# A transformer block with a product-key expert layer on one core: later searches queued behind the latest weighting, transposes of places set apart, block 0's places loaded during attention

## The chip, the core and the metric

The kernel runs on one core of a Trainium2 chip. The core has five engines, each with a queue of its own: PE (TensorE, matrix products and transposes; its weight loads are shown as PEld), DVE (VectorE), ACT (ScalarE), POOL (GpSimd) and SP (SyncE, which here issues nearly all DMAs). PE writes into PSUM, eight banks of 128 partitions x 2 KB; the others work between SBUF and PSUM. The metric is the device time of one execution in microseconds, the median of several runs.

## What is computed

N = 2048 tokens of width D = 448, one layer of attention (16 heads of 28) and one of experts, each behind a normalization and added to its input:

```
h  = x + softmax(q k^T / sqrt(28)) v @ wo          with q, k, v from layernorm(x) @ wqkv
xf = layernorm(h)
q1, q2 = halves of xf @ w_q                        (16 heads, 256 each)
s1, s2 = q1 @ k1^T, q2 @ k2^T                      (64 keys each)
t1, i1 = the 8 largest of s1;  t2, i2 = the 8 largest of s2
top_s, top_e = the 8 largest of the 64 sums t1 + t2, with expert numbers 64 * i1 + i2
g = softmax(top_s)
out = sum over heads and k of g * gelu(xf . u[top_e]) * v[top_e]       (4096 experts)
h2 = h + out
```

## The kernel before

The token axis is cut into four blocks of 512 tokens (b = 0 to 3), each of four groups of 128 (j). Instead of gathering rows of u and v for each token, the kernel computes all 4096 experts for all tokens, in 32 slices f of 128 experts, and multiplies by a dense matrix G of weights that is zero where an expert wasn't chosen. Products are made of half-precision parts (a high and a low part of each factor), so an up-projection of one slice and block is 11 matmuls of 128x512 (`mm_all`, L92) and the weighted sum is 12 matmuls of 128x448 per slice (L1194).

**Stages.** First the projections for q, k, v. Then attention, in 257 steps of a Python generator; into the same stretch are woven, by hand, the projection, the scores and the search for the best keys of token blocks 0, 1 and 2, and the splitting of u and v into parts. Then a short stage that projects block 3, keeps its key scores for later (`kept_scores`, in the 16 tiles `ring`) and builds the weights G of block 0. Then four expert blocks, one for each token block.

**Weaving.** `weave((generator, n, lo, hi), ...)` runs generators in turn: the n units of a generator get evenly spaced places between lo and hi, and the unit with the smallest place is traced next. A unit is what a generator does up to its next `yield`; an empty unit only takes a place.

**Queues.** Up to the end of the weights of block 0 the order of the woven text is the order of the queues (`manual_schedule`). In the expert blocks a compile-time scheduler orders each engine's queue: of the instructions that it takes to be ready, the first in the text. `tc.issue_after(ins)` forbids it to put what is traced inside ahead of `ins` on the engine of `ins`; it adds no wait at run time, and it binds only that engine's instructions.

**An expert block** (`experts`, L1172): 32 steps. Step f traces the up-projection of a slice some way ahead (`up`, PE then ACT's gelu, L1153, into one of four tiles of `ring` in block 0, of twenty later), the weighting of slice f+2 (`weigh`: DVE multiplies the gelu's result by G, L1167; ACT makes the high half of it, L1168; DVE makes the low half, L1169) and the 12 matmuls of slice f into the four PSUM banks `acc` (L1194). Blocks 1 to 3 begin with 19 up-projections made ahead (`ups`).

**Weights** (`weights(b)`, L936): loads the chosen places of block b from DRAM (`st` from `sd`, L940, its first unit), then for 32 chunks of 16 tokens makes on DVE indicator matrices (f1 L952, fg L958, p L973; two buffers of p, tag p1) and on PE their products (L1000 for block 0; L990 for the others), which go to G (L1002, or L993 on ACT and L994 on DVE). Of block b+1, the first chunks (EARLY: 11, 8, 11) are made during expert block b and the rest at the start of expert block b+1.

**Later searches** (`later`, L1210): what remains of the search is done in the expert blocks. In order: `pairs_of` for groups 2 and 3 of token block 2 (9 units each; the best 8 of 64 sums, with `found`: four times MAX8, L796, and four times FIND_INDEX8, L798, in a unit, then index arithmetic), `places_of` block 2 (9 units: `soften` on DVE and ACT, then `to_slots`: for each of four groups four transposes on PE, L903, into a PSUM tile of name M of which there are two, and two copies by ACT, L96 in the profile, then a store to `sd`), `bests` of block 3 (32 units of `found` on the kept scores), `pairs_of` for the four groups of block 3 and `places_of` block 3. LATER gives the units for expert blocks 0, 1 and 2, and SPLIT the share of the block over which they are spread; the first units of the next block's weights take the rest. All of them stand inside `behind(newest[0], ...)`, where `newest[0]`, read once when `later` is made, is the last p instruction of block 0's weights.

Of the kernel before, what the change touches and what calls it, by code (L numbers as in the profile page):

```python
# [60 lines left out]
def block(ctx: ExitStack, tc: tile.TileContext, x, wqk, wv, wo, wq, k12, uT, v, cst, out):  # L61
# [811 lines left out]
    PAIRS = 9  # L873
# [20 lines left out]
            if j % 2:  # L894
                yield

    def to_slots(eng, b):
        st = bg.tile([128, 2, 1024], F16, name="st", bufs=2)
        slots, gslots = st[:, 0].rearrange("p (k n) -> p k n", k=2), st[:, 1].rearrange("p (t k u) -> p t k u", k=2, u=2)
        for j in range(4):  # L900
            p = P[0].tile([128, 4, 128], F16, name="M")
            for k in range(4):
                nc.tensor.transpose(p[:, k], sl[j][:, k], ident16)  # L903
            copy(eng, slots[:, :, 128 * j:128 * j + 128], p[:, :2])
            copy(eng, gslots[:, 64 * j:64 * j + 64], p[:, 2:].rearrange("p k (t u) -> p t k u", u=2))
            yield
        nc.sync.dma_start(s_d[b], st)

    def places_of(b, eng):
        yield from soften()  # L910
        yield from to_slots(eng, b)

    PLACES = 9

# [5 lines left out]
    def behind(ins, gen):  # L920

        while True:
            with tc.issue_after(ins):
                if next(gen, end) is end:
                    return
            yield
# [130 lines left out]
    with tc.manual_schedule(engines={ET.PE, ET.DVE, ET.Activation, ET.Pool, ET.SP}):  # L1057
# [28 lines left out]
        for b in range(3):  # L1086
            t = begin[b] - FOLDED
            look = search(b, [(i, j) for g in ((0, 1), (2, 3)) for i in range(4) for j in g])
            work += [(project(b), PROJECT, t, t + PROJECT), (islice(look, 1), 1, t + 20, t + 21)]
            t += 26  # L1090
            p = 64 * b + 175 - FOLDED
            work += [(look, SEARCH, t, t + SEARCH)]
            if b < 2:
                work += [(chain(*[pairs_of(j, nc.gpsimd) for j in range(4)]), 4 * PAIRS_POOL, t + 18, p),
                         (places_of(b, nc.scalar), PLACES, p, p + 12)]
            else:
                work += [(pipeline([pairs_of(j, nc.gpsimd) for j in (0, 1)], 6), 6 + PAIRS_POOL, t + 20, 257 - FOLDED)]
        work += [(parts_of_up(14, 32), 18 + PART, 0, 40), (tops(VS, lambda f: v[:, f], D), TOPS, 6, 66), (VS.share(), 3, 67, 70), (scales(), 1, 73, 74),
                 (parts_of_down(0, 14), 14 + PART, 74, 120), (parts_of_down(14, 32), 18 + PART, 120, 180)]
        weave(*work)  # L1100
# [16 lines left out]
    with tc.manual_schedule(engines={ET.PE, ET.DVE, ET.Activation, ET.Pool, ET.SP}):  # L1117
        room = {"xt": [ring[4 * j + 2] for j in range(4)], "at": [ring[3], ring[7]]}
        pools = [tc.tile_pool(name="sw0", bufs=1, side="right", reuse_waits="tile")]
        with ExitStack() as c1:  # L1120
            pools = [c1.enter_context(pools[0])]
            w0, sc = weights(0), kept_scores(3, pools)
            weave((project(3, 2, room), 12, 0, 0.25), (islice(w0, 1), 1, 0.01, 0.02), (islice(sc, 1), 1, 0.02, 0.03),
                  (islice(w0, 8), 8, 0.05, 0.27), (islice(sc, 4), 4, 0.125, 0.29))
            r2.close()
            be = ctx.enter_context(tc.tile_pool(name="be", bufs=3, reuse_waits="tile"))
            c2 = c1.enter_context(ExitStack())
            pools.append(c2.enter_context(tc.tile_pool(name="sw1", bufs=1, reuse_waits="tile")))
            next(sc)

            def loads():
                store_X(3)
                yield
                for f in range(3):
                    us[f] = load_u(f)
                    yield

            weave((w0, WEIGHTS - 9, 0.29, 1), (sc, 13, 0.29, 0.92), (loads(), 4, 0.6, 0.8))
            load_X(0)
# [21 lines left out]
    def weigh(b, f):  # L1161
        vt = bv.tile([128, 3, D], F16, name="v")
        nc.sync.dma_start(vt, vs_d[f])
        a = acts.pop(f)
        w = gw.tile([128, 2, 512], F16, name="w", tag=f"wr{f % 2}")
        av = a.rearrange("p (c t) -> p c t", t=TG) if b % 2 else a
        nc.vector.scalar_tensor_tensor(av, av, wscale, of_expert(b, f), op0=OP.mult, op1=OP.mult)  # L1167
        nc.scalar.activation(w[:, 0], a, AF.Copy, scale=1.0 / LS)  # L1168
        nc.vector.scalar_tensor_tensor(w[:, 1], w[:, 0], -LS, a, op0=OP.mult, op1=OP.add)  # L1169
        return w, [vt[:, k] for k in range(3)]  # L1170

    def experts(b, n, acc):  # L1172
# [33 lines left out]
            yield  # L1206

    AHEAD = 19
    dr = iter(())
    later = behind(newest[0], chain(pairs_of(2, nc.vector), pairs_of(3, nc.vector), places_of(2, nc.scalar), bests(), *[pairs_of(j, nc.vector) for j in range(4)], places_of(3, nc.scalar)))  # L1210
    EARLY = {1: 11, 2: 8, 3: 11}
    SUMMED = {b: set(range(32)) for b in EARLY}
    LATER = (2 * PAIRS + PLACES + 32, 3 * PAIRS, PAIRS + PLACES + 1)
    SPLIT = (0.58, 0.5, 0.3)
    tag = ["A"]
    ws = None
    for b in range(NB):
# [61 lines left out]
```

## Time and profile before

| | |
|---|---|
| runs | 1620.35, 1622.07, 1620.88 us; median 1620.88 |
| profiled execution | 1622.36 us in all, span of its instructions 1620.6 us |
| mean granted clock of PE | 0.993 |
| moved by DMA | 263.36 MB, mean 163 GB/s |

A row of a group in the profile has line, engine, operation, output and inputs, shapes, count, busy time and mean. A row in order of time has start (us), duration (us), engine, line, operation and, in brackets, the idle time before it and what ended it. A row of stretches has begin and end, length, busy us and count of PE, PEld, DVE, ACT and POOL, then the granted clock of PE, the DMA engines' busy share and GB/s. [...]

### The profile page before, as it was taken

The numbers are of one execution on the slowest core, as the hardware profiler recorded it, in microseconds if no ns is written. First come the engines' busy times: TensorE is split into PE (matmuls) and PEld (weight loads), VectorE is DVE, ScalarE is ACT, GpSimd is POOL, SyncE is SP. The second block draws the span as 40 slices with busy tenths as digits, with TensorE's granted clock in tenths as the row PEclk, the third lists the DMA queues.
The fourth block names the chain that finished last, engine by engine and source line by source line (L and its number), as shares of the span: only waits on it lengthen the run. The fifth ranks groups of instructions, "written<-read, shape, count | busy, mean of one in ns | idle before, by whom it ended". The sixth has DMA issues, their size and how long they took to land.

```text
span 1620.6 us, 33317 instructions
## 1 busy us (share of the span) xinstructions
PE 1553.8 (96%) x12585; PEld 676.6 (42%) x12585; DVE 1144.8 (71%) x3875; ACT 932.0 (58%) x1272; POOL 364.9 (23%) x488
## 2 busy tenths in 40 slices
PE   5999999999999999999997998999999999999999
PEld 3444222233333333233335654455545554555444
DVE  8763442645576667565597999959998899779732
ACT  3544878999888888888883433233423344334322
POOL 1241003556213575487542000000000000000000
PEclk9999999999999999999999999999999999999999
DMA  8424874777853476357623234444344433454353
GB/s 282 135 98 134 289 238 157 235 254 258 290 175 102 126 257 211 119 164 238 196 84 116 97 109 145 129 123 152 108 135 137 158 108 115 153 159 126 113 151 127
DMA packets 158882, 263.36 MB, mean 163 GB/s; under 512 B 14336, under 2 KB 90880, under 8 KB 158720
## 3 DMA queue, kind: packets, MB, share of 16 engines
q1 hardware_dynamic: 154496, 259.12, 50.0%
q10 hardware_dynamic: 4224, 2.10, 0.4%
q8 instruction: 99, 1.62, 0.4%
q14 instruction: 63, 0.52, 0.1%
HBM read 211.88 MB, written 49.28 MB: 161 GB/s over the span
## 4 chain that ended last, share of the span: by engine, by line
PE 74%; DVE 17%; DMA 3%; ACT 3%; issue 2%; POOL 1%; SPq 0%; DVEq 0%; POOLq 0%
PE acc L1194 16%; PE M L92 13%; PE A L590 12%; PE S L564 11%; PE A L92 9%; PE pq L92 6%; DVE p L973 4%; DVE G L994 2%; DVE fg L958 2%; ACT P L568 2%; PE M L262 1%; PE A L1000 1%; DVE f L952 1%; PE M L121 1%; DVE ti L798 1%
## 5 line engine op out<-in xcount | busy, mean ns | idle before, releaser
L568 ACT ACTIVATE P<-S,escale 128x1024 f32<-128x1024 f32 x512 | 534.6, 1132 | 70.6 <-PE S L564 70.6
L1194 PE MATMUL acc<-v,w 128*128 128x448 f16 x1536 | 306.5, 353 | 0.0
L590 PE MATMUL A<-P,V 128*32 128x512 f32 x2048 | 263.8, 604 | 0.0
L564 PE MATMUL S<-qS,kS 32*128 32x512 f16 x3072 | 238.6, 379 | 3.8 <-ACT P L568 2.2
L1194 PEld LDWEIGHTS <-w 128*128 128x128 f16 x1536 | 149.1, 98 | 142.2 <-issue 2.6
L1168 ACT ACTIVATE w<-ring 128x512 f16<-128x512 f32 x128 | 80.6, 630 | 206.8 <-PE acc L1194 108.4
L92 PEld LDWEIGHTS <-u 128*128 128x128 f16 x1408 | 133.3, 98 | 150.7 <-issue 9.8
L973 DVE TENSOR_TENSOR p<-st,iota 128x2048 f16<-128x2048 f16 x128 | 155.5, 1216 | 7.7 <-PE A L1000 4.1
L564 PEld LDWEIGHTS <-kS 32*128 32x128 f16 x3072 | 65.6, 92 | 205.5 <-issue 168.7
L92 PE MATMUL A<-XHb,u 128*128 128x512 f16 x568 | 137.9, 386 | 4.0 <-DVE G L994 3.8
L1169 DVE SCALAR_TENSOR_TENSOR w<-w,ring 128x512 f16<-128x512 f16 x128 | 86.9, 685 | 66.0 <-ACT w L1168 66.0
L92 PE MATMUL M<-w,XHb 128*128 128x512 f16 x512 | 127.9, 380 | 2.8 <-DVE oh L128 1.5
L1167 DVE SCALAR_TENSOR_TENSOR ring<-ring,wscale,G 128x512 f32<-128x512 f32 x128 | 92.5, 743 | 34.7 <-ACT ring L1153 34.5
L92 PE MATMUL M<-XHb,u 128*128 128x512 f16 x456 | 110.9, 379 | 0.8 <-DVE G L994 0.8
L1153 ACT ACTIVATE ring<-A,ugelu 128x512 f32<-128x512 f32 x71 | 48.6, 684 | 89.5 <-PE A L92 89.5
L590 PEld LDWEIGHTS A<-P,V 128*32 128x32 f32 x2048 | 45.6, 108 | 114.3 <-issue 108.5
L796 DVE MAX8 ti<-fresh 128x8 f32<-128x64 f32 x384 | 57.2, 211 | 50.5 <-ACT fresh L777 50.1
L1153 ACT ACTIVATE ring<-M,ugelu 128x512 f32<-128x512 f32 x57 | 39.2, 688 | 81.7 <-PE M L92 81.5
L853 POOL TENSOR_TENSOR sel<-sel,iv 128x256 f16<-128x256 f16 x80 | 54.6, 715 | 133.5 <-DVE sel L849 133.5
L1030 POOL TENSOR_SCALAR raw<-raw,scale 128x512 f32<-128x512 f32 (+1 forms) x64 | 45.5, 711 | 157.1 <-DMA raw<-in_uT_dram 132.2
L958 DVE TENSOR_TENSOR fg<-f,st 128x2048 f16<-128x2048 f16 x64 | 77.8, 1215 | 0.1
L798 DVE FIND_INDEX8 ti<-ti,fresh 128x8 uint32<-128x64 f32 x384 | 76.8, 219 | 0.0
(199 smaller groups left out, 2096.0 us busy)
## 6 DMA issues: line engine op xcount, KB each, us to landing
v<-vs SPq DMA_DIRECT2D x128, 336.0 KB, 2.8
u<-us SPq DMA_DIRECT2D x128, 256.0 KB, 2.6
w<-wp SPq DMA_DIRECT2D x56, 512.0 KB, 5.4
kS<-ks SPq DMA_DIRECT2D x64, 256.0 KB, 4.7
V<-vd SPq DMA_DIRECT2D x64, 256.0 KB, 2.8
raw<-in_uT_dram SPq DMA_DIRECT2D x64, 256.0 KB, 5.3
wr<-in_wq_dram SPq DMA_DIRECT2D x32, 448.0 KB, 4.2
raw<-in_v_dram SPq DMA_DIRECT2D x64, 224.0 KB, 5.1
```

The source lines that it names most:

```text
L92: nc.tensor.matmul(ps, l, r, start=i == 0, stop=i == len(pairs) - 1)
L564: nc.tensor.matmul(S[j // 2][:, j % 2], kS[r, a, 128 * (k % 4):128 * (k % 4) + 128], qS[r, c], start=m == 0, stop=m == 2)
L568: nc.scalar.activation(Pt[:, 2 * i:2 * i + 2], S[i], AF.Exp, scale=escale[:, n % 4:n % 4 + 1])
L590: nc.tensor.matmul(O[n][32 * j:32 * j + 32], V[:, k % 4, j], Pt[:, j], start=k == 0, stop=k == NT - 1)
L798: nc.vector.max_index(i, t, src)
L958: nc.vector.tensor_tensor(fg.rearrange("p t k f u -> p t k (f u)"), f1.rearrange("p t f u -> p t (f u)").unsqueeze(2).to_broadcast([128, T ...
L973: newest[0] = nc.vector.tensor_tensor(p1, pairs(0, s, TG, 128), ids(TG, 128), op=OP.is_equal).ins
L1153: nc.scalar.activation(act, p, AF.Gelu_apprx_tanh, scale=ugelu)
L1167: nc.vector.scalar_tensor_tensor(av, av, wscale, of_expert(b, f), op0=OP.mult, op1=OP.mult)
L1168: nc.scalar.activation(w[:, 0], a, AF.Copy, scale=1.0 / LS)
L1169: nc.vector.scalar_tensor_tensor(w[:, 1], w[:, 0], -LS, a, op0=OP.mult, op1=OP.add)
L1194: nc.tensor.matmul(acc[j][:, :D], l, r, start=f == 0 and k == 0, stop=f == 31 and k == 2)
```

## The change

Three edits. (1) `weights(0)` is created before the weave of attention, and its first unit, the load of `st`, gets place 220 to 221 of attention's 257 instead of a place at the start of the next stage. (2) `to_slots` takes a `gap`: after each group of transposes and copies it yields gap + 1 times; GAP is 3 for token block 2 and 0 elsewhere, so expert block 0 has 71 units of later searches instead of 59, and SPLIT for it is 0.65 instead of 0.58. (3) `behind` gets the list `newest` and reads it at every unit, and `weigh` writes its second DVE instruction (L1169) there. So each unit of the later searches, in all expert blocks, goes behind the newest weighting (or the newest p of `weights`) that has been traced.

```diff
-    def to_slots(eng, b):
+    def to_slots(eng, b, gap=0):
...
             copy(eng, gslots[:, 64 * j:64 * j + 64], p[:, 2:].rearrange("p k (t u) -> p t k u", u=2))
-            yield
+            for _ in range(gap + 1):
+                yield
         nc.sync.dma_start(s_d[b], st)
 
-    def places_of(b, eng):
+    def places_of(b, eng, gap=0):
         yield from soften()
-        yield from to_slots(eng, b)
+        yield from to_slots(eng, b, gap)
...
         while True:
-            with tc.issue_after(ins):
+            with tc.issue_after(ins[0]):
                 if next(gen, end) is end:
                     return
             yield
...
+        w0 = weights(0)
+        work += [(islice(w0, 1), 1, 220 - FOLDED, 221 - FOLDED)]
...
-            w0, sc = weights(0), kept_scores(3, pools)
-            weave((project(3, 2, room), 12, 0, 0.25), (islice(w0, 1), 1, 0.01, 0.02), (islice(sc, 1), 1, 0.02, 0.03),
+            sc = kept_scores(3, pools)
+            weave((project(3, 2, room), 12, 0, 0.25), (islice(sc, 1), 1, 0.02, 0.03),
                   (islice(w0, 8), 8, 0.05, 0.27), (islice(sc, 4), 4, 0.125, 0.29))
...
-        nc.vector.scalar_tensor_tensor(w[:, 1], w[:, 0], -LS, a, op0=OP.mult, op1=OP.add)
+        newest[0] = nc.vector.scalar_tensor_tensor(w[:, 1], w[:, 0], -LS, a, op0=OP.mult, op1=OP.add).ins
...
     AHEAD = 19
+    GAP = 3
     dr = iter(())
-    later = behind(newest[0], chain(pairs_of(2, nc.vector), pairs_of(3, nc.vector), places_of(2, nc.scalar), bests(), *[pairs_of(j, nc.vector) for j in range(4)], places_of(3, nc.scalar)))
+    later = behind(newest, chain(pairs_of(2, nc.vector), pairs_of(3, nc.vector), places_of(2, nc.scalar, GAP), bests(), *[pairs_of(j, nc.vector) for j in range(4)], places_of(3, nc.scalar)))
...
-    LATER = (2 * PAIRS + PLACES + 32, 3 * PAIRS, PAIRS + PLACES + 1)
-    SPLIT = (0.58, 0.5, 0.3)
+    LATER = (2 * PAIRS + PLACES + 4 * GAP + 32, 3 * PAIRS, PAIRS + PLACES + 1)
+    SPLIT = (0.65, 0.5, 0.3)
```

## The prediction

> **What bounds the kernel now.** I read the page first (spans and shares), then busy time by stretches, then the instructions of each engine in order of time around the three places that the change touches.
>
> ```profile
> span 1620.6 us, 33317 instructions
> PE 1553.8 (96%) x12585; PEld 676.6 (42%) x12585; DVE 1144.8 (71%) x3875; ACT 932.0 (58%) x1272; POOL 364.9 (23%) x488
> ```
>
> PE is busy for 96% of the span, so there are 67 us of idle PE to win or to add to, plus what PE does at a lowered clock. Busy time by stretches (PE, PEld, DVE, ACT, POOL, then granted clock):
>
> ```profile
> 850.00:948.00 98.00, 84.99 (x1297) 57.37 (x1291) 82.31 (x110) 37.41 (x62) 12.51 (x20) 0.97 0.32 105
> 948.00:1047.00 99.00, 94.07 (x474) 44.93 (x471) 98.09 (x582) 32.19 (x53) 0.00 (x0) 0.95 0.43 132
> 1047.00:1100.00 53.00, 53.00 (x346) 27.12 (x345) 30.45 (x46) 18.86 (x36) 0.00 (x0) 1.00 0.45 138
> 1100.00:1172.60 72.60, 69.26 (x680) 38.61 (x679) 72.60 (x126) 28.90 (x72) 0.00 (x0) 1.00 0.39 122
> 1172.60:1230.00 57.40, 57.38 (x292) 28.29 (x290) 57.40 (x226) 17.43 (x28) 0.00 (x0) 1.00 0.43 132
> ```
>
> The first row is the stage between attention and experts (the projection of block 3, its kept scores, the weights of block 0). The second and third are expert block 0: DVE is full (98.09 of 99) while it does the later searches beside the weighting, then idles for 22.5 us of 53. From 1100 to 1172.6 DVE is full and sets the pace, with PE idle 3.3 us. The last row is the head of expert block 1: both full.
>
> **First places loaded in attention.** Before, the load of block 0's places is issued when attention has ended, and DVE waits for it:
>
> ```profile
> 853.72 0.69 DVE L595 COPY o<-A 128x512 f32<-128x512 f32 x1 [2.81 <-PE A L590]
> 857.81 0.29 DVE L128 TENSOR_TENSOR oh<-M,oh 64x128 fp32r<-64x128 f32 x1
> 860.61 0.69 DVE L952 TENSOR_TENSOR f<-st,iota 128x1024 f16<-128x1024 f16 x1 [2.52 <-DMA st<-sd]
> 862.48 1.22 DVE L973 TENSOR_TENSOR p<-st,iota 128x2048 f16<-128x2048 f16 x1
> ```
>
> ```profile
> 859.93 0.78 PE L92 MATMUL M<-woh,ol 128*128 128x448 f32 x3
> 863.75 1.04 PE L1000 MATMUL A<-fg,p 128*128 128x32 f16 x32 [3.05 <-DVE p L973]
> ```
>
> DVE's three instructions move from 860.61 to 858.1 and PE's from 863.75 to about 861.25; PE is free from 860.7, so the whole 2.5 us reach the path. The chain behind (transposes, projections, DVE, PE) hangs on these, and the other loads of the stage land earlier than needed. I take **-2.5 us**; the bounds are 0 (another input late by as much) and -5.4: in the stretch after the wait the clock was halved,
>
> ```profile
> 859.40:862.80 3.40, 1.31 (x7) 0.87 (x5) 2.15 (x3) 1.14 (x2) 0.00 (x0) 1.00 0.83 255
> 862.80:869.60 6.80, 5.84 (x47) 5.08 (x47) 5.41 (x9) 1.19 (x2) 1.98 (x2) 0.50 0.38 132
> 992.50:995.90 3.40, 0.63 (x3) 0.20 (x2) 3.40 (x34) 0.00 (x0) 0.00 (x0) 1.00 0.33 101
> 995.90:1002.70 6.80, 4.82 (x15) 2.00 (x15) 6.71 (x54) 3.07 (x8) 0.00 (x0) 0.50 0.20 78
> ```
>
> and 5.84 busy us at half clock hold 2.9 us that a full clock would save, if PE's quiet 3.4 us before it (1.31 busy) fill up. At its new place the step issues one DMA of 512 KB, and its source was written long before:
>
> ```profile
> L907 SPq DMA_DIRECT2D sd<-st x4: 319/320/382, 668.4 to 1376.8; - x4
> L940 SPq DMA_DIRECT2D st<-sd x4: 320/403/434, 856.5 to 1379.8; - x4
> ```
>
> ```profile
> L568 ACT ACTIVATE P<-S,escale 128x1024 f32<-128x1024 f32 x512 | 534.6, 1132 | 70.6 <-PE S L564 70.6
> ```
>
> Block 0's places are stored at 668.4. Attention's 257 steps end with the copy of o at 853.7 (above); each has two exponentials of 1.13 us, so step 220 lies at least 37 x 2.26 = 84 us earlier, before 770. SP's queue waits for nothing there, and the K, V and query loads behind it are fetched pieces ahead: no cost. The buffers of the places (two) turn in another order, but each is read out before its next writer.
>
> [...] The rows have halved stretches of 6.8 us, each behind a stretch of 3.4 us in which PE was at most 39% busy. [...]
>
> **Transposes of places apart.** In block 0 the four groups of four transposes (L903) come one unit apart, through two PSUM buffers; the third and fourth need ScalarE's copies of the first and second:
>
> ```profile
> 991.99 0.50 PE L903 MATMUL M<-ident,sl 128*128 128x128 f16 x6
> 997.88 0.59 PE L903 MATMUL M<-ident,sl 128*128 128x128 f16 x4 [4.75 <-ACT st L96]
> 1001.68 2.96 PE L1194 MATMUL acc<-v,w 128*128 128x448 f16 x12
> ```
>
> ```profile
> 996.65 0.63 ACT L1168 ACTIVATE w<-ring 128x512 f16<-128x512 f32 x1 [4.38 <-DVE ring L1167]
> 997.19 1.97 ACT L96 ACTIVATE st<-M 128x256 f16<-128x256 f16 x6
> ```
>
> The copies stand in ACT's queue behind a weighting copy, that behind DVE's weighting, that behind searches; matmuls of a started group stand behind the transposes on PE. The stall costs 4.75 us idle, and the half-clock stretch 995.9 to 1002.7 (above) costs half of its 4.82 busy us, 2.4: together **-7.2 us**. With GAP 3 the groups are four units apart, 4 x 0.65 x 32 / 71 = 1.17 steps of an expert; a step of PE is 4.64 us:
>
> ```profile
> 1009.12 1.89 PE L92 MATMUL A<-XHb,u 128*128 128x512 f16 x8
> 1013.76 1.89 PE L92 MATMUL A<-XHb,u 128*128 128x512 f16 x8
> ```
>
> So 5.4 us lie between groups and 10.9 between users of one buffer, and no search unit follows the last group before its own gap. I take the stall as gone; the bounds are -7.2 and 0 for this term.
>
> **Units behind the latest weighting.** The 59 search units may no longer be issued on DVE before the second half (L1169) of the newest weighting. Prices per unit and per weighting:
>
> ```profile
> 948.85 0.60 DVE L796 MAX8 ts<-cand 128x8 f32<-128x64 f32 x4
> 950.14 0.59 DVE L796 MAX8 ts<-cand 128x8 f32<-128x64 f32 x4
> 1046.73 0.75 DVE L1167 SCALAR_TENSOR_TENSOR ring<-ring,wscale,G 128x512 f32<-128x512 f32 x1
> 1048.17 0.69 DVE L1169 SCALAR_TENSOR_TENSOR w<-w,ring 128x512 f16<-128x512 f16 x1 [0.69 <-ACT w L1168]
> 1048.78 0.75 DVE L1167 SCALAR_TENSOR_TENSOR ring<-ring,wscale,G 128x512 f32<-128x512 f32 x1
> ```
>
> A search unit is 1.28 us (948.85 to 950.14); a weighting is 2.05, of which DVE works 1.36 and waits 0.69 for ScalarE. Before, that wait is filled with search units:
>
> ```profile
> DVE w L1169 <- ACT w L1168: 0.7, 1, 0.7
> ```
>
> that is one wait of 0.7 us in 948 to 1047, for 19 weightings. Now only the first half of the next weighting can fill it, if its gelu is there. The units come denser while they come: 71 (12 of them empty) in 20.8 steps, 3.41 a step. In the last part, 32 units in 9.4 steps, DVE then needs 3.41 x 1.28 + 1.36 = 5.7 us a step, 6.4 with the wait unfilled; PE needs 9.4 x 4.64 plus two extra up-projections of 2.37, 48.3 us in all. DVE falls behind by 5.5 to 12 us. It may be late by what separates a weighting from its use:
>
> ```profile
> 959.86 0.68 DVE L1169 SCALAR_TENSOR_TENSOR w<-w,ring 128x512 f16<-128x512 f16 x1
> 966.38 2.43 PE L1194 MATMUL acc<-v,w 128*128 128x448 f16 x12
> ```
>
> 5.8 us (966.38 - 960.54; weighting 2). So PE waits 0 to 6 us there. In the first part, 18 units of pairs, 5.3 steps are 24.5 us of PE. DVE's 98.09 busy us less 19 to 20 weightings (26.5) and 6 of early weights leave 65.6 for 59 units, 41 of it for the 32 of the last part, 3 for softening, so 21.6 for the pairs; 21.6 + 5.3 x (1.36 to 2.05) = 28.8 to 32.5: late by 4 to 8 us against 5.8, a wait of 0 to 2. The softening follows late as well, and PE takes its instructions in order, so the first transposes can wait for DVE as they now wait for ACT, 0 to 4.75 (the nearest row). In between the empty units let DVE catch up. Together 0 to 13; I take the low side, **+2 us**, because DVE kept pace before with 98% of work and a full half of these waits can be filled from step 12 on, where gelus run ahead.
>
> In blocks 1 and 2 the gelus are 19 ahead, so the next weighting's first half always fills the wait; DVE is full and PE waits for nothing until 1230: 0, within 1 us.
>
> **The split.** The 13 first units of block 1's weights now lie in 0.67 to 1 of the block instead of 0.60 to 1: at step 27.5 five of the eleven chunks are through instead of six. A chunk on DVE:
>
> ```profile
> 1132.63 0.74 DVE L994 TENSOR_TENSOR G<-A,G 128x256 f32<-128x256 f32 x2
> 1133.30 0.68 DVE L952 TENSOR_TENSOR f<-st,iota 128x1024 f16<-128x1024 f16 x1
> 1133.90 1.22 DVE L973 TENSOR_TENSOR p<-st,iota 128x2048 f16<-128x2048 f16 x1
> 1135.03 1.21 DVE L958 TENSOR_TENSOR fg<-f,st 128x2048 f16<-128x2048 f16 x1
> ```
>
> 0.67 + 1.13 + half of 0.60 and of 1.14, 2.67 us. Since DVE has no pause from 1100 to 1172.6, a chunk more behind step 27 comes back as PE waiting. The idle 22.5 us ahead of it don't help, as two buffers of p let DVE run only two chunks ahead. Searches that end later also leave fewer weightings done ahead, up to two (2.7). Bounds 0 and 5.4; I take **+3 us**.
>
> **Sum.** -2.5 - 7.2 + 2 + 3 = -4.7 us. The profiled execution's span of 1620.6 becomes 1615.9. Its own time was 1622.36, which is 1.5 above the median of the runs; the median 1620.88 becomes 1616.2. Likeliest case's own range: 1612 to 1620.
>
> **The rivals.** (1) The queue is too strict, and it is slower: the wait of 0.69 stays unfilled, the stall at the transposes is replaced by PE waiting for DVE, at the transposes and at the weighted sums. It decides from about 5.9 us of DVE a step. Price: 13 - 7.2 - 2.5 + 3 = +6.3, 1627. For it: DVE is full already in that stretch; against it: the units per step rise only from 3.18 to 3.41. [...] (2) The start also keeps its clock and the tail has room: -5.4 - 7.2 + 1 + 1, 1610. For it: PE's first gap shrinks from 3.05 to 0.6 us; against it: DVE was at 82 of 98 us in that stage and the tail has none to spare. (3) The stall goes, but all of it comes back in 1100 to 1172.6, where DVE is the bound: -2.5 - 7.2 + 4 + 5.4, 1620.5, nothing to be seen.
>
> **How the numbers follow.** Forecast 0.46, rival 1 0.24, rival 2 0.12, rival 3 0.18. This kernel's measurement tells 0.2% (3.2 us) from no change: faster is below 1617.6, slower above 1624.1. The forecast's range lies three quarters on the faster side (0.35, 0.11 same); rival 2 is faster, rival 3 mostly the same (0.04 faster, 0.13 same, 0.01 slower), rival 1 slower (0.23, 0.01 same). Faster 0.51, same 0.25, slower 0.24. The range goes from rival 2 to just short of rival 1: 1610 to 1626.
>
> **What would show it.** In the changed profile: no row of DVE waiting for st after 854, and L1000's first group near 861; the wait of L903 for ACT gone and the clock 1.00 throughout block 0; DVE's wait for L1168 grown from 0.7 to between 5 and 15 us in block 0; waits of PE for L1169 or for sl of at most 2 us; the first chunk's G at about step 23.5 and PE's waits for G between 1100 and 1170 up by some 3 us. The forecast is wrong if PE waits more than 5 us for DVE inside block 0, if the stall reappears at the transposes, or if the stage after attention doesn't get shorter by 2 us.

## The result and the profile after

The changed kernel takes 1631.99 us (median of 6 runs, 1628.73 to 1633.93) against 1621.47 for the kernel before in the same runs: a ratio of 1.0055, 95% interval 1.0041 to 1.0069, so 9 us slower (the two medians are 10.5 us apart) where 4.7 us faster were forecast. Its profiled execution took 1631.04 us. The page begins with the span and the shares:

```profile
span 1629.1 us, 33319 instructions
PE 1555.5 (95%) x12585; PEld 675.7 (41%) x12585; DVE 1143.2 (70%) x3875; ACT 932.5 (57%) x1272; POOL 363.8 (22%) x488
```

The work of every engine is what it was; the span has grown by 8.5 us, so the question is only where PE stands still or runs at half clock. The line numbers of the changed kernel: f L953, fg L959, p L974, G L995, first chunk's products L1001, gelu L1156, the weighting L1170 (first half), L1171 (ScalarE's copy), L1172 (second half), weighted sum L1197.

**Where the time went.** The table gives the time between points that both traces have: the last copy of o (o), and the first matmul of the weighted sum of slice f in block b, written b.f. It is worked out from the start of those instructions.

| us | to o | o to 0.0 | to 0.9 | to 0.20 | to 0.27 | to 0.31 | to 1.0 | to 2.0 | to 2.9 | to the end |
|---|---|---|---|---|---|---|---|---|---|---|
| before | 853.7 | 103.4 | 49.8 | 56.2 | 35.4 | 11.0 | 64.7 | 171.8 | 32.0 | 242.6 |
| after | 853.1 | 100.0 | 48.1 | 56.5 | 44.3 | 12.1 | 65.9 | 171.4 | 35.2 | 242.5 |

The start gained 3.4 us, the transposes' stretch (0.0 to 0.9) 1.7. Slices 20 to 27 of block 0 lost 8.9, the tail 1.1 + 1.2, and the last transposes' stretch of block 2 lost 3.2. Busy time by stretches, columns as in the prediction (PE, PEld, DVE, ACT, POOL, clock):

```profile
850.00:948.00 98.00, 86.03 (x1318) 57.13 (x1311) 84.04 (x116) 38.75 (x63) 12.03 (x19) 0.98 0.32 103
948.00:1047.00 99.00, 94.85 (x469) 45.60 (x468) 82.70 (x424) 31.64 (x51) 0.00 (x0) 0.98 0.45 135
1047.00:1100.00 53.00, 46.98 (x270) 22.62 (x269) 40.21 (x181) 15.96 (x30) 0.00 (x0) 0.90 0.35 104
1100.00:1178.40 78.40, 74.55 (x730) 41.65 (x729) 77.84 (x120) 32.53 (x78) 0.00 (x0) 1.00 0.42 129
```

In the first 99 us of block 0 DVE worked 98.09 us before and 82.70 now. Of the 15 us that it didn't work there, 10 came in 1047 to 1100 (40.21 instead of 30.45) and the rest later, and in 1047 to 1100 PE is idle for 6 us and its clock is down to 0.90. The waits of PE in block 0 (total, times, longest):

```profile
PE A L92 <- ACT ring L1156: 6.0, 3, 3.5
PE M L903 <- DVE sl L892: 4.2, 1, 4.2
```

Before, L903 waited 4.75 us for ScalarE's copy. Now it waits 4.2 us for `sl`, which DVE makes at the end of the softening, and a wait for gelus has appeared.

**The wait for `sl`** begins at the head of the block. DVE, then PE (rows of DVE overlap by some 0.08 us; before, 1048.17 + 0.69 ends at 1048.86 and the next starts at 1048.78):

```profile
949.29 0.75 DVE L1170 SCALAR_TENSOR_TENSOR ring<-ring,wscale,G 128x512 f32<-128x512 f32 x1 [3.09 <-ACT ring L1156]
951.67 0.75 DVE L1170 SCALAR_TENSOR_TENSOR ring<-ring,wscale,G 128x512 f32<-128x512 f32 x1 [1.62 <-ACT ring L1156]
955.49 0.69 DVE L1172 SCALAR_TENSOR_TENSOR w<-w,ring 128x512 f16<-128x512 f16 x1 [0.70 <-ACT w L1171]
961.38 0.69 DVE L1172 SCALAR_TENSOR_TENSOR w<-w,ring 128x512 f16<-128x512 f16 x1 [0.69 <-ACT w L1171]
973.90 0.69 DVE L1172 SCALAR_TENSOR_TENSOR w<-w,ring 128x512 f16<-128x512 f16 x1 [0.69 <-ACT w L1171]
```

```profile
988.86 0.29 PE L903 MATMUL M<-ident,sl 128*128 128x128 f16 x1 [4.15 <-DVE sl L892]
```

The first search unit starts at 956.10, behind the third weighting; until then DVE only weighs and waits for gelus, where before it searched from 948.85 on (a row of the prediction). Three waits of 0.7 us for ScalarE's copy (0.70 + 0.69 + 0.69 = 2.1) stand unfilled before the softening.

**The start** did what was foreseen. DVE in order of time (start, duration), then PE:

```profile
853.11 0.69 DVE L595 COPY o<-A 128x512 f32<-128x512 f32 x1 [2.81 <-PE A L590]
857.20 0.29 DVE L128 TENSOR_TENSOR oh<-M,oh 64x128 fp32r<-64x128 f32 x1
857.52 0.69 DVE L953 TENSOR_TENSOR f<-st,iota 128x1024 f16<-128x1024 f16 x1
859.50 1.21 DVE L974 TENSOR_TENSOR p<-st,iota 128x2048 f16<-128x2048 f16 x1
```

```profile
860.77 0.97 PE L1001 MATMUL A<-fg,p 128*128 128x32 f16 x32 [0.64 <-DVE p L974]
```

From the copy of o to L1001 it is now 7.66 us (860.77 - 853.11) where it was 10.03 (863.75 - 853.72), and f follows L128 without a wait.

**The wait for gelus** is read from three queues between 1046 and 1070. DVE:

```profile
1048.02 1.39 DVE L1170 SCALAR_TENSOR_TENSOR ring<-ring,wscale,G 128x512 f32<-128x512 f32 x2
1049.44 0.69 DVE L1172 SCALAR_TENSOR_TENSOR w<-w,ring 128x512 f16<-128x512 f16 x1
1053.90 0.67 DVE L1172 SCALAR_TENSOR_TENSOR w<-w,ring 128x512 f16<-128x512 f16 x1
1059.62 1.39 DVE L1170 SCALAR_TENSOR_TENSOR ring<-ring,wscale,G 128x512 f32<-128x512 f32 x2
```

ACT:

```profile
1048.78 1.29 ACT L1171 ACTIVATE w<-ring 128x512 f16<-128x512 f32 x2 [6.86 <-DVE ring L1170]
1049.98 1.25 ACT L1156 ACTIVATE ring<-A,ugelu 128x512 f32<-128x512 f32 x2
1060.39 1.35 ACT L1171 ACTIVATE w<-ring 128x512 f16<-128x512 f32 x2 [9.16 <-DVE ring L1170]
1061.65 0.67 ACT L1156 ACTIVATE ring<-A,ugelu 128x512 f32<-128x512 f32 x1
1068.22 0.63 ACT L1171 ACTIVATE w<-ring 128x512 f16<-128x512 f32 x1 [5.90 <-DVE ring L1170]
1068.76 0.67 ACT L1156 ACTIVATE ring<-A,ugelu 128x512 f32<-128x512 f32 x1
```

PE:

```profile
1052.42 0.81 PE L92 MATMUL A<-XLb,u 128*128 128x512 f16 x3
1055.34 1.89 PE L92 MATMUL A<-XHb,u 128*128 128x512 f16 x8
1057.07 0.81 PE L92 MATMUL A<-XLb,u 128*128 128x512 f16 x3
1057.71 2.43 PE L1197 MATMUL acc<-v,w 128*128 128x448 f16 x12
1062.37 2.31 PE L92 MATMUL A<-XHb,u 128*128 128x512 f16 x8 [2.22 <-ACT ring L1156]
1064.48 1.49 PE L92 MATMUL A<-XLb,u 128*128 128x512 f16 x3
1069.48 3.57 PE L92 MATMUL A<-XHb,u 128*128 128x512 f16 x8 [3.52 <-ACT ring L1156]
1072.85 1.35 PE L92 MATMUL A<-XLb,u 128*128 128x512 f16 x3
```

The first halves of two weightings stand side by side (x2 at 1048.02), then come the two second halves with three and four search units behind them, and only at 1059.62 the next pair. ACT's copies come in pairs too, 9.16 us of idle time apart. The gelus follow in the order of the up-projections: the two at 1049.98 read up-projections that ended before 1049, and the one at 1061.65 reads the up-projection that PE ended at 1053.23 (1052.42 + 0.81). It stands in ACT's queue behind the pair of copies and starts 8.4 us after its input was ready. The next up-projection, ended at 1057.88 (1057.07 + 0.81), gets its gelu only at 1068.76, behind the copy at 1068.22. These up-projections turn through two PSUM tiles, and a tile isn't free until a gelu has read it: so the up-projection at 1062.37 waits 2.22 us for the first of these gelus, and the one at 1069.48 waits 3.52 for the second. The clock falls as well, to 0.50 from 1063.69 to 1073.93: the eleven matmuls of an up-projection, 2.54 us from 1055.34 on (1057.88 - 1055.34), take 3.60 from 1062.37 on and 4.72 from 1069.48 on. Idle 2.22 + 3.52 and 1.06 + 2.18 of slower matmuls make 9.0 us, about the 8.9 that the stretch 0.20 to 0.27 lost. Waits for gelus are not the tie's alone, though: the experiments below find nearly as much of them without it.

The gelu didn't pass the copies: ACT idled for 9.16 us up to 1060.39, with the gelu's input ready for the last 7.2 of them (1060.39 - 1053.23), and did the copies first.

### The profile page after: what moved, and what is told of

It reads as the page before. It is cut to its first block, busy times and chain, and to the rows that moved or that the text cites. A ratio compares the mean times of both kernels' runs of the same rounds, so it can differ in the third digit from the quotient of the medians.

```text
span 1629.1 us, 33319 instructions
## 1 busy us (share of the span) xinstructions
PE 1555.5 (95%) x12585; PEld 675.7 (41%) x12585; DVE 1143.2 (70%) x3875; ACT 932.5 (57%) x1272; POOL 363.8 (22%) x488
## 4 chain that ended last, share of the span: by engine, by line
PE 70%; DVE 19%; DMA 4%; ACT 3%; POOL 2%; issue 2%; SPq 0%; DVEq 0%; POOLq 0%; ACTq 0%
PE acc L1197 16%; PE M L92 11%; PE A L590 11%; PE S L564 11%; PE A L92 8%; PE pq L92 5%; DVE p L974 4%; DVE G L995 2%; DVE ti L798 2%; ACT P L568 2%; DVE fg L959 2%; DMA w<-wp 2%; PE M L262 2%; DVE ti L796 1%; PE A L1001 1%
## 5 line engine op out<-in xcount | busy, mean ns | idle before, releaser
L1197 PE MATMUL acc<-v,w 128*128 128x448 f16 x1536 | 307.8, 354 | 0.0
L1197 PEld LDWEIGHTS <-w 128*128 128x128 f16 x1536 | 149.1, 98 | 141.9 <-issue 3.2
L1171 ACT ACTIVATE w<-ring 128x512 f16<-128x512 f32 x128 | 80.4, 630 | 208.7 <-PE acc L1197 107.9
L974 DVE TENSOR_TENSOR p<-st,iota 128x2048 f16<-128x2048 f16 x128 | 155.5, 1216 | 7.7 <-PE A L1001 4.1
L564 PEld LDWEIGHTS <-kS 32*128 32x128 f16 x3072 | 65.5, 92 | 204.7 <-issue 168.3
L1172 DVE SCALAR_TENSOR_TENSOR w<-w,ring 128x512 f16<-128x512 f16 x128 | 87.3, 687 | 68.4 <-ACT w L1171 66.7
L1170 DVE SCALAR_TENSOR_TENSOR ring<-ring,wscale,G 128x512 f32<-128x512 f32 x128 | 92.0, 745 | 41.2 <-ACT ring L1156 41.0
L1156 ACT ACTIVATE ring<-A,ugelu 128x512 f32<-128x512 f32 x71 | 48.4, 683 | 92.0 <-PE A L92 92.0
L1156 ACT ACTIVATE ring<-M,ugelu 128x512 f32<-128x512 f32 x57 | 39.2, 687 | 76.8 <-PE M L92 76.6
L959 DVE TENSOR_TENSOR fg<-f,st 128x2048 f16<-128x2048 f16 x64 | 77.9, 1217 | 0.2
```

What stands on the lines that cost most here:

```text
L564: nc.tensor.matmul(S[j // 2][:, j % 2], kS[r, a, 128 * (k % 4):128 * (k % 4) + 128], qS[r, c], start=m == 0, stop=m == 2)
L959: nc.vector.tensor_tensor(fg.rearrange("p t k f u -> p t k (f u)"), f1.rearrange("p t f u -> p t (f u)").unsqueeze(2).to_broadcast([128, T ...
L974: newest[0] = nc.vector.tensor_tensor(p1, pairs(0, s, TG, 128), ids(TG, 128), op=OP.is_equal).ins
L1156: nc.scalar.activation(act, p, AF.Gelu_apprx_tanh, scale=ugelu)
L1172: newest[0] = nc.vector.scalar_tensor_tensor(w[:, 1], w[:, 0], -LS, a, op0=OP.mult, op1=OP.add).ins
L1197: nc.tensor.matmul(acc[j][:, :D], l, r, start=f == 0 and k == 0, stop=f == 31 and k == 2)
```

## The experiments

Twelve kernels ran, each beside the kernel before on the same chip. Times are medians; the ratio is to the kernel before. The last four columns are the stretches of the table above in each kernel's profiled execution. A profiled execution can lie off the median: that of `no_gap` took 1631.25 us, that of `tie_b0` 1626.86. `pool_copy` and `late_first` have 4 runs, `tie_b0` 5, the others 10.

| kernel | us | ratio, 95% interval | o to 0.0 | to 0.9 | to 0.20 | to 0.27 |
|---|---|---|---|---|---|---|
| load_only | 1621.58 | 0.9987 (0.9976 to 0.9998) | 102.8 | 49.8 | 56.1 | 35.4 |
| no_tie | 1622.54 | 0.9996 (0.9985 to 1.0008) | 100.0 | 42.2 | 65.2 | 35.0 |
| no_gap | 1626.62 | 1.0022 (1.0009 to 1.0034) | 101.5 | 48.9 | 60.7 | 35.4 |
| pool_copy | 1637.72 | 1.0097 (1.0072 to 1.0122) | 98.4 | 50.5 | 56.7 | 38.3 |
| tie_first | 1621.46 | 0.9994 (0.9985 to 1.0004) | 100.2 | 44.7 | 58.7 | 37.8 |
| tie_b0 | 1630.57 | 1.0042 (1.0027 to 1.0057) | 100.1 | 48.3 | 56.5 | 44.4 |
| filled | 1628.46 | 1.0036 (1.0026 to 1.0046) | 100.1 | 45.7 | 61.8 | 36.6 |
| late_part | 1618.91 | 0.9976 (0.9966 to 0.9986) | 101.5 | 42.0 | 61.1 | 35.4 |
| late_nogap | 1622.21 | 0.9995 (0.9985 to 1.0005) | 99.7 | 42.7 | 66.3 | 35.4 |
| late_first | 1615.93 | 0.9952 (0.9935 to 0.9970) | 98.5 | 42.7 | 58.9 | 35.4 |
| first_58 | 1624.65 | 1.0012 (1.0000 to 1.0023) | 99.7 | 49.1 | 60.6 | 35.4 |
| late_free | 1621.51 | 0.9991 (0.9981 to 1.0000) | 101.5 | 41.9 | 65.5 | 35.4 |

**One edit or two of the three.** `load_only` is the kernel before with edit 1 alone; `no_tie` has edits 1 and 2 without the tie; `no_gap` has edits 1 and 3 without the places set apart:

```diff
# no_tie, against the changed kernel: the list is copied, so that it never changes
-    later = behind(newest, chain(
+    later = behind(newest[:], chain(
# no_gap, against the changed kernel
-    GAP = 3
+    GAP = 0
-    SPLIT = (0.65, 0.5, 0.3)
+    SPLIT = (0.58, 0.5, 0.3)
```

> Kernel before with the first edit alone: block 0's places are loaded at step 220 of attention. In the changed kernel the way from attention's last copy of o (L595) to the first weighted sum (L1194) is 100.0 us against 103.4 before, with the clock at 1.00 behind it. Theory: this edit is a gain of its own, 3.4 us, carried to the end: 1618.0 against 1621.5, the stall at the transposes as before (4.7 us). Rival: the gain is lost again at the first point where VectorE sets the pace (1100 to 1172 in the profile before): way from attention to the first weighted sum shorter, time within 1 us of before.

> The changed kernel with the third edit taken back: the later searches stand behind the last p of block 0's weights again, GAP 3, SPLIT 0.65 and the early load stay. Theory (the tie is the loss): VectorE's 16 idle us of block 0's first 99 us go back under 3 us, TensorE's waits for gelus (L1153, 6.0 us and half clock after them) and for sl at the transposes of blocks 0 and 2 (4.2 and 2.3 us) are gone, the stall at the transposes of before too: 1621.5 - 3.4 - 7 + 2 = 1613. Rival (density: 71 units and empty places in 0.65 of the block press the searches together): the gelu waits stay over 4 us with the tie gone, 1626 to 1630.

> The changed kernel with the second edit taken back: GAP 0 and SPLIT 0.58, the early load and the tie stay. Theory (the tie makes VectorE idle and late, the gap only sets where): no empty units, so VectorE idles less, the searches end earlier; gelu waits of 2 to 6 us, and the transposes wait for sl by 3 to 5 us, in part for ScalarE's copies as before: 1624 to 1629. Rival (gap and split are the loss): gelu waits under 1 us, 1618 to 1620.

`load_only` gained 0.13%, 2.1 us (by its interval 0.3 to 3.9), which agrees with the 2.5 us that the wait for `st` took and lies between the two expectations. In its profiled execution, though, the stretch from o to 0.0 is only 0.6 us shorter than before: the wait is gone, but the clock was halved at other places, one of them here:

```profile
855.56:858.97 3.41, 1.55 (x9) 1.31 (x10) 2.17 (x5) 0.60 (x1) 2.98 (x6) 1.00 0.53 138
858.97:862.38 3.41, 3.41 (x23) 2.73 (x22) 2.52 (x3) 0.73 (x2) 0.18 (x1) 0.50 0.82 296
```

`no_tie` shows what setting the transposes apart, with the longer split, is worth: nothing that its interval can tell (0.9996, against 0.9987 for `load_only`). The stretch 0.0 to 0.9 fell from 49.8 to 42.2 us, the 7 us of the prediction, and the next one rose from 56.2 to 65.2. DVE is without a pause from 955 to 1015, and PE, which had waited once for 4.75 us, now waits five times for a gelu, 5.5 us in all:

```profile
955.00:1015.00 60.00, 57.96 (x294) 27.97 (x293) 60.00 (x374) 19.32 (x34) 0.00 (x0) 1.00 0.47 146
```

```profile
PE A L92 <- ACT ring L1156: 5.5, 5, 2.0
```

DVE's 98 us of work in those 99 us set the pace before as well; the stall lay in their shadow. Neither expectation held in full: the gelu waits stayed over 4 us, as the rival had it, but the time is neither near 1613 nor within 1626 to 1630. `no_gap` fell where the theory had it (1624 to 1629): the tie alone makes the kernel slower, by 0.35% against `load_only` (1.0022 to 0.9987). The tie on top of the two other edits costs 0.59% (1.0055 to 0.9996), 9.6 us.

**What in the tie costs.** Two theories were tested: the paired copies on ACT hold the gelus up; or DVE loses time because a tied unit can't run while the newest weighting waits for its gelu. DVE's waits between 948 and 1047 in the changed kernel, where before there was one of 0.7 us for L1168:

```profile
DVE ring L1170 <- ACT ring L1156: 11.7, 6, 3.1
DVE w L1172 <- ACT w L1171: 4.2, 6, 0.7
```

`pool_copy` takes the copies off ACT; `tie_first` ties to the first half, so that the 0.7 us in which L1172 waits can be filled with units again, and not with the next first half; `tie_b0` leaves the units of blocks 1 and 2 behind block 0's last weighting, so that there they may run ahead as before; `filled` puts bests into the empty units:

```diff
# pool_copy
-        nc.scalar.activation(w[:, 0], a, AF.Copy, scale=1.0 / LS)
+        nc.gpsimd.tensor_scalar(w[:, 0], a, 1.0 / LS, 1.0, op0=OP.mult, op1=OP.mult)
# tie_first
-        nc.vector.scalar_tensor_tensor(av, av, wscale, of_expert(b, f), op0=OP.mult, op1=OP.mult)
+        newest[0] = nc.vector.scalar_tensor_tensor(av, av, wscale, of_expert(b, f), op0=OP.mult, op1=OP.mult).ins
-        newest[0] = nc.vector.scalar_tensor_tensor(w[:, 1], w[:, 0], -LS, a, op0=OP.mult, op1=OP.add).ins
+        nc.vector.scalar_tensor_tensor(w[:, 1], w[:, 0], -LS, a, op0=OP.mult, op1=OP.add)
# filled
-    places_of(2, nc.scalar, GAP), bests(),
+    soften(), spaced(to_slots(nc.scalar, 2), bests(), GAP),
```

> The changed kernel with the weighting's copy (w[:, 0], L1171) made by GpSimd instead of ScalarE, in all blocks. Theory (the gelus wait because they stand in ScalarE's queue behind that copy, which waits for VectorE): TensorE's waits for gelus in block 0 fall from 6.0 us under 1 us, VectorE is as late as before, first weighted sums wait for it by 0 to 3 us instead: 1622 to 1627, unless GpSimd's copy is slower than 1 us. Rival (VectorE simply has too much to do there, whatever stands in ScalarE's queue): the same waits come back at the weighted sums (L1197), 1630 to 1633.

> The changed kernel with the units tied to the first half of the newest weighting (L1170) instead of its second (L1172), so that VectorE may search while ScalarE makes the copy. Theory A (what the tie costs is mostly this unfilled wait of 0.7 us a weighting, in the first part of block 0): VectorE's idle in block 0's first 99 us falls from 16 to 8 us or less, and 3 to 6 us come back: 1625 to 1628. Theory B (the empty units between the groups of transposes are what leaves VectorE idle, and the tie keeps it from searching there): idle stays over 12 us, 1630 to 1633.

> The changed kernel with the tie in expert block 0 alone: from block 1 on the units stand behind block 0's last weighting and may be issued ahead again. Both theories: the wait of the transposes for sl in block 2 (2.3 us and half clock behind it) is gone and the way from block 2's first to its tenth weighted sum is 32.0 us again instead of 35.2: 1628 to 1629 against 1632. If it were not the tie, it would stay at 35.

> The changed kernel with the three empty units behind each group of transposes filled by searches of block 3 (bests), 59 units over 0.65 of block 0, tie as in the changed kernel. Theory B: VectorE's idle in block 0's first 99 us falls from 16 to 6 us or less, TensorE's waits for gelus from 6.0 to under 1.5 us: 1621 to 1624. Theory A: the idle only falls to 11 or so, gelu waits of 3 to 6 us stay: 1627 to 1630.

`pool_copy` is a miss as a cure and a hit as a probe. PE waits for no gelu in block 0 any more, and the stretch 0.20 to 0.27 fell from 44.3 to 38.3 us, as it must if the copies ahead of the gelus are what PE waits for there. But GpSimd's copy comes back later (mean 801 ns in block 0 against ScalarE's 630), so L1172 waits for it, the softening is later still, and the whole is slower, most of it in blocks 1 and 2 (1.0 to 2.9 takes 215.4 us instead of 206.6):

```profile
DVE w L1172 <- POOL w L1171: 15.0, 23, 0.8
```

```profile
PE M L903 <- DVE sl L892: 9.1, 2, 5.2
```

`tie_first` gives back 0.61% (1.0055 to 0.9994), 9.9 us, more than either expectation had. ACT's copies come singly again:

```profile
1044.42 0.63 ACT L1171 ACTIVATE w<-ring 128x512 f16<-128x512 f32 x1 [5.18 <-DVE ring L1170]
1049.53 0.63 ACT L1171 ACTIVATE w<-ring 128x512 f16<-128x512 f32 x1 [3.33 <-DVE ring L1170]
1055.91 0.63 ACT L1171 ACTIVATE w<-ring 128x512 f16<-128x512 f32 x1 [5.18 <-DVE ring L1170]
```

Its longest wait of ACT for L1170 is 5.2 us between 1000 and 1080, against 4.5 before and 9.2 in the changed kernel. DVE's idle time is hardly cured by it (86.30 busy of 99 us), and the waits for gelus are hardly fewer:

```profile
PE A L92 <- ACT ring L1156: 5.0, 3, 2.7
PE M L903 <- DVE sl L892: 2.0, 1, 2.0
```

So PE waits 5 to 6 us for gelus in block 0 with the pairs (6.0), with copies that come singly as before (5.0) and with no tie at all (5.5 in `no_tie`). What fell is the longest such wait, from 3.5 to 2.7 us, and the wait for `sl`, by 2.2 us, as much as the three unfilled waits before the softening, which `tie_first` doesn't have. The clock stays at 1.00 from 0.0 to 1.0, where in the changed kernel it is 0.96 in 0.0 to 0.9 and 0.88 in 0.20 to 0.27. `tie_b0` recovered in its profiled execution what block 2 had lost (2.0 to 2.9 takes 32.6 us instead of 35.2) and nothing of block 0 up to 0.31; the medians say 2.1 us, with intervals that overlap. In block 2, too, the transposes wait for `sl`, in the changed kernel

```profile
PE M L903 <- DVE sl L892: 2.3, 1, 2.3
```

and 0.9 in `tie_b0`. `filled` stayed within the pairing theory's 1627 to 1630: with units in the empty places DVE is busy for 86.84 of the 99 us, as much as in `tie_first`, but a pair of copies is still there, with 8.5 us of idle time behind it. Of these two with the same idle time of DVE `tie_first` is 7 us faster, but half of that lies in block 2 (2.0 to 2.9 takes 31.7 us against 35.2). That the pairing makes most of the loss is not shown.

What the tie costs in block 0 is best read against `no_tie`, which differs in nothing else. From 0.0 to 1.0, the changed kernel first:

```profile
953.12:1179.97 226.85, 212.83 (x1448) 108.25 (x1447) 200.21 (x721) 78.32 (x156) 0.00 (x0) 0.97 0.41 125
954.24:1173.67 219.43, 209.70 (x1445) 106.93 (x1443) 193.03 (x694) 77.36 (x156) 0.00 (x0) 0.99 0.44 130
```

It is 7.4 us longer: PE is idle for 4.3 us more (14.0 against 9.7), as much as its wait for `sl` (4.2), and busy for 3.1 us more with the same work, at a lower clock. In block 2 it is the wait for `sl` again (3.1 us from 2.0 to 2.9). The share that the pairs have, through the two longer gelu waits around which the clock was 0.50 (1063.69 to 1073.93), stays open: no run takes away the pairs alone.

**Room for the stall's gain.** If DVE is the bound of block 0's first 100 us and idles 22 us afterwards, searches should go from the one to the other. `late_part` leaves the first 20 bests untied in their place, gives the last 12 a place of their own in 0.5 to 0.85 of the block, tied to the newest second half, and has SPLIT 0.58. `late_nogap` is the same with GAP 0. `late_first` puts 18 bests there, from 0.45, and ties them to the first half; `late_free` is `late_first` without that tie. `first_58` is `tie_first` with the old SPLIT.

```diff
# late_part, against the changed kernel
-    later = behind(newest, chain(pairs_of(2, nc.vector), pairs_of(3, nc.vector), places_of(2, nc.scalar, GAP), bests(), ...
+    bs = bests()
+    tail = behind(newest, bs)
+    later = behind(newest[:], chain(pairs_of(2, nc.vector), pairs_of(3, nc.vector), places_of(2, nc.scalar, GAP), islice(bs, 20), ...
+        if b == 0:
+            work += [(tail, 12, 0.5, 0.85)]
# late_first, against late_part, beside the edit of tie_first
-islice(bs, 20)
+islice(bs, 14)
-            work += [(tail, 12, 0.5, 0.85)]
+            work += [(tail, 18, 0.45, 0.85)]
# late_free, against late_first
-    tail = behind(newest, bs)
+    tail = behind(newest[:], bs)
```

> The early load and GAP 3 with SPLIT 0.58, no tie for the first 20 of the 32 searches of block 3, and the last 12 of them (15 us of VectorE) in a weave of their own at 0.5 to 0.85 of block 0, each behind the newest weighting. Theory (VectorE's load up to 1047 sets the pace of block 0, with or without a stall at the transposes, and its 22 idle us behind are free): TensorE's gelu waits fall under 1 us, the way from block 0's first to its last weighted sum is 144 to 147 us against 152.4 before: 1613 to 1616. Rival (the late searches only move the wait into 1047 to 1172, where VectorE has to make the weights): block 0 shorter by 6 us, the stretch to block 1's first sum longer by as much: 1620 to 1622.

> late_part with GAP 0, so that the four groups of transposes stand one unit apart again (47 units in 0.58 of the block, the last 12 bests as in late_part). Theory: the stall at the transposes was free before only because VectorE was the bound of the first 100 us of block 0; with 12 units moved to the later part VectorE has some 7 us to spare there, so the stall now costs: 3 to 6 us above late_part, 1622 to 1625, with a wait of the transposes (L903) for a copy or for sl of 4 us or more and a stretch of half clock near it. Rival: what the stall leaves is made up for by the searches here too, and the time is within 1.5 us of late_part (1617.5 to 1620.5).

> late_part with 18 of the 32 bests in the later part (0.45 to 0.85 of the block) instead of 12, and the tie of this later part to the first half of the newest weighting (L1170) instead of the second. Theory: VectorE's work per step is then nearly even over the block and ScalarE's copies come singly, not in pairs: gelu waits of PE below 2 us in block 0, 2 to 4 us below late_part, 1615 to 1617. Rival: the stretch from 0.9 to 0.20 was already bound by PE, and the later searches now meet the first chunks of block 1's weights: the same as late_part or up to 3 us above (1618.5 to 1622).

> late_first with the tie of its 18 later bests taken away: all units again stand only behind the last p of block 0's weights, as in the kernel before, and only their places in the text hold them. If the tie is what keeps the weightings evenly spaced: the scheduler brings some of the 18 forward and PE waits again, 2 to 4 us above late_first, 1618 to 1620. If the places alone make late_first's gain and the tie is worth nothing there: within 1.5 us of late_first, 1614.5 to 1617.5.

> tie_first with SPLIT 0.58 instead of 0.65: only the split is undone (searches denser, block 1's first weight units from 0.60). The term of the prediction: 3 us less than tie_first, 1618.5. The theory now: 1.1 us less at the end of block 0 and up to 1 us at the head of block 1, but the 71 places come 12% denser where VectorE is full and give back as much: within 1.5 us of tie_first, 1620 to 1623.

`late_part` beats both kernels, 0.24% under the one before, though by less than was expected: PE still waits 3.5 us for gelus where under 1 was forecast. DVE has room now in the first 99 us and works more in the next 53, and PE doesn't stop from 1047 to 1100, as in the kernel before:

```profile
948.00:1047.00 99.00, 94.96 (x469) 45.23 (x468) 92.06 (x505) 33.22 (x55) 0.00 (x0) 0.99 0.45 134
1047.00:1100.00 53.00, 53.00 (x374) 27.73 (x372) 38.82 (x120) 18.19 (x37) 0.00 (x0) 1.00 0.46 139
```

`late_nogap` is 0.19% (3.1 us) above it, the intervals barely touching (0.9986 and 0.9985 at their ends), and its stall is back and counts: the stretch to 0.20 is 66.3 us instead of 61.1. It is a larger stall than that of the kernel before, two waits instead of one of 4.75 us.

```profile
PE M L903 <- ACT st L96: 6.9, 2, 4.6
```

So setting the transposes apart is worth something once DVE isn't the bound: 3 us between the medians, 5.9 us in these stretches of the profiled executions (42.7 + 66.3 against 42.0 + 61.1). Moving the 12 units without it gained nothing either: `late_nogap` is at 0.9995, `load_only` at 0.9987. `late_first` is the fastest by its 4 runs, 1615.93 us, 0.48% under the kernel before. Its interval overlaps with that of `late_part`, and a gain over it can't be placed: from 0.0 to 1.0 the two take 214.4 and 214.6 us, and the 3 us between their starts (98.5 and 101.5) go with the clock (1.00 and 0.96 from 850 to 948), not with the edit. Its one wait for a gelu is short, and ACT's longest wait for L1170 is 4.8 us:

```profile
PE A L92 <- ACT ring L1156: 0.8, 1, 0.8
```

`late_free` loses 0.39% (6.3 us) against it, more than was expected; 4.2 us of that show from 0.0 to 1.0 of the profiled executions (218.6 against 214.4), with 5.8 us of such waits again and DVE at 95.98 of 99 us: without the tie the scheduler takes the 18 units as soon as DVE is free, as before. The tie that the change introduces is thus worth having there, on the right half. `first_58` missed: undoing the split was expected to change nothing, and the prediction's term said a gain of 3; it came out 0.18% (2.9 us) above `tie_first`, with intervals that overlap a little. From 0.20 to 0.31 it is 3.5 us shorter, but the stretches to 0.9 and to 0.20 grew by 4.4 and 1.9, where the units now come denser.

## Why the prediction was wrong, step by step

- **What bounds block 0.** The view of stretches stood there with DVE at 98.09 of 99 us, and the prediction read it as a full engine beside the path. `no_tie` shows that it was the path, and `late_part`, which takes 12 units away from it, gains.
- **The stall, -7.2: the first failed step.** Its size was right (0.0 to 0.9 fell by 7.6 us in `no_tie`), its worth was not: "I take the stall as gone; the bounds are -7.2 and 0 for this term", and the bound of 0 held. The step never asked what DVE would be late with once PE stopped waiting; the answer was five waits for gelus, 5.5 us, and in all 9.0 us more for the next 11 slices (65.2 against 56.2). In the changed kernel the stall took a new form besides, 4.2 us for `sl`, within the "0 to 4.75" that the prediction had for it.
- **The tie, +2: the second.** The measured price is 9.6 us, within the bounds of 0 and 13 and far from the value taken. The terms that were taken low came in part: the transposes waited 4.2 us for DVE, where 0 to 4.75 had been allowed, and again in block 2, where nothing had. That PE did nothing past a waiting transpose is in the trace before: of an up-projection it did three matmuls at 992.32 and the other eight only from 998.26 on, behind the transposes that had waited 4.75 us. The step that failed reads "a full half of these waits can be filled from step 12 on, where gelus run ahead". More than half of the loss in block 0, the wait for `sl`, was made before step 12, at the head of the block and in the three waits left unfilled ahead of the softening; later the waits were filled with the next first half, which pairs the weightings and makes PE's longest wait for a gelu 3.5 us instead of 2.0. The waits at the weighted sums that made up 6 of the 13 didn't come at all; PE waited for gelus, a chain through ACT's queue and two PSUM tiles that the prediction's slack of 5.8 us, counted from DVE to the weighted sum, left out. Nor has the tie's term anything for the clock, which was 0.97 from 0.0 to 1.0 against 0.99 in `no_tie`, with 3.1 us more of busy PE for the same work.
- **The first load, -2.5:** right in mechanism and size. The copy of o to L1001 shrank by 2.4 us; `load_only` measured 2.1. The further 1 us in the changed profile goes with the clock, which was 1.00 from 850 to 900 there, 0.93 before and 0.86 in `load_only`. All thirteen kernels with this edit have the same program up to the expert blocks, and in their profiled executions the clock there differs: from 850 to 900 it was 1.00 in the changed kernel (100.0 us from o to 0.0) and 0.86 in `load_only` (102.8), from 850 to 948 it was 1.00 in `late_first` (98.5), 0.96 in `late_part` (101.5) and 0.95 in `late_nogap`, `first_58` and `late_free` (99.7, 99.7 and 101.5).
- **The split, +3:** `first_58` and `tie_first` differ in it alone. The tail pays 2.4 + 1.1 us for it (0.20 to 0.31), about what the term says, but the step weighed the tail alone: spreading the units also relieves the stretch ahead, there by 6.3 us, more than the tail pays. The 1.2 us more from 0.31 to 1.0 aren't the split's but go with the tie of block 1: the stretch takes 64.7 to 65.0 us in every kernel without that tie, whatever its split, and 65.9 to 67.6 in every one with it.
- **Blocks 1 and 2, "0, within 1 us":** wrong by 3.2 us in block 2, where the softening stands behind weightings as well and the transposes wait for it; the profile of `tie_b0` has it undone. Block 1 held (171.4 against 171.8) but for the 1.2 us at its head.
- **The rivals.** Rival 1, +6.3, had the sign and came nearest, with the transposes waiting for DVE as it said; its reason, a wait of 0.69 us left unfilled, holds for 2.1 of those 4.2 us, and the weighted sums that it named didn't wait. Rival 2's start, with the clock kept, is what the profiles of the changed kernel (1.00 from 850 to 900) and of `late_first` (1.00 from 850 to 948) show; its tail isn't. Rival 3, the stall's gain all given back, is what `no_tie` did, only that it came back in slices 9 to 20 and not behind 1100.
- **What would have shown it.** "If PE waits more than 5 us for DVE inside block 0" named the wrong engine: PE waited 4.2 us for DVE and 6.0 for ACT, which waited for DVE. The second sign, the stall reappearing at the transposes, did come.

By the profiled stretches: -0.6 to o, -3.4, -1.7, +0.3, +8.9, +1.1, +1.2, -0.4, +3.2, -0.1 make +8.5, the 8.5 between the spans.

## What to carry to other kernels

A stall of the main engine inside a stretch in which another engine is full is not time to be won: move work of the full engine to where it idles, and take the stall away with it (here neither gained anything alone, and together they were 3 us better than either). When a scheduling constraint is put on a queue, ask first what can no longer start early, here the searches at the head of the block, then what the scheduler will put into the holes that are left, and follow both through every queue they touch up to the resource that is freed last, here ACT's copies, the gelus and two PSUM tiles. Which of two instructions a constraint names can matter more than whether there is one: the same tie cost 9.6 us on the second half of the weighting, about nothing on the first, and gained 6 there with the units spread to where VectorE was idle.

## What was unexpected of the hardware

Whether the start of the stage after attention ran at half clock differed between kernels that have the same program up to there (0.86 from 850 to 900 in `load_only`, 1.00 in the changed kernel). In the traces of the kernel before and of the changed kernel the clock changes only at points that are multiples of 3.41 us apart (halved from 862.79 to 869.62, 948.13 to 951.54 and 995.91 to 1002.74 before; from 944.22 to 947.64, 988.60 to 992.01 and 1063.69 to 1073.93 in the changed kernel), and where these points lie differs between the two executions. In `load_only` a window of 3.41 us with 1.55 us of busy PE was followed by half clock (rows above), so such a window doesn't have to be idle for it. In the changed kernel the windows fall otherwise, none between 850 and 900 holds less than 1.83 us, and the clock stays at 1.00:

```profile
872.54:875.95 3.41, 1.83 (x10) 0.89 (x11) 3.28 (x7) 0.60 (x1) 0.00 (x0) 1.00 0.01 2
875.95:879.36 3.41, 3.41 (x74) 2.77 (x73) 3.33 (x6) 1.73 (x3) 0.74 (x2) 1.00 0.20 72
```

In the profiled executions of the kernel before and of the changed kernel (from 100 to 1600 us, windows at full clock) each of the 6 windows with less than 1.5 us of busy PE was followed by half clock, 3 of the 17 from there to 2.2 us, and none of the 841 above. A gain of 1 to 3 us at such a place isn't to be read from one profile of each kernel.
